# Windowed attention and a feed-forward block on one core: local units taken one by one, or in pairs

## The chip, the core and the metric

The program runs on one core of a Trainium2 chip. A core has a matrix engine (TensorE, in the profile PE, its weight loads PEld), a vector engine (VectorE, DVE), an engine for activation functions (ScalarE, ACT), a general one (GpSimd, POOL), and a queue from which all transfers of this program are issued (SyncE, SP; the transfers themselves are DMAs). Each engine works through its own list of instructions in order and waits at semaphores for the others. The metric is the device time of one execution in microseconds (us); lower is better.

## The reference

```python
# q_l, k_l, v_l: (8, 8, 512, 64); q_g, k_g, v_g: (8, 8, 32, 64), float32
def sm(s):
    e = np.exp(s - np.max(s, axis=-1, keepdims=True))
    return e / (np.sum(e, axis=-1, keepdims=True) + 1e-09)
k_all, v_all = concat([k_g, k_l]), concat([v_g, v_l])
out_g = sm(scale * q_g @ k_all.T) @ v_all               # 32 global rows see all 544
s_ll = np.where(abs(i - j) <= 32, scale * q_l @ k_l.T, -1e9)
a_l = sm(concat([scale * q_l @ k_g.T, s_ll]))           # 512 local rows see a band and the globals
out_l = a_l @ v_all
x = concat([out_g, out_l], axis=2).transpose(0, 2, 1, 3).reshape(8, 544, 512)
xn = (x - mean(x)) / sqrt(var(x) + 1e-06) * g_ln
return x + np.maximum(xn @ w_ch1, 0) @ w_ch2            # 512 -> 2048 -> 512
```

## The kernel before, in words

The feed-forward block (`ffn`) runs over nine chunks. Chunks 0 to 7 hold 512 local rows each (one batch), the last one the 256 global rows. A chunk goes through 16 slices f of the hidden layer. `mm1(f)` is 12 matrix products of 128 rows by 512 columns into a PSUM tile `ph` (each operand is split in a high and a low part, `xh`, `xl`, `w`; three of the four products are made); ScalarE then writes `hh` (L540, the high part of the rectified result) and VectorE `hl` (L541, the low part). `mm2(f - 1, t)` for four row tiles t is 12 more products from the `hh` and `hl` of the slice before into four accumulators `acc`. So a slice is 24 products, a chunk 384, and the `hl` of slice f is first needed after `mm1(f + 1)`.

The attention of the next chunk is pushed between these products. A unit (`Local`) is one batch, two heads and half of the local rows; a chunk needs 8 units. A unit's steps are: `scores`, small products into two tiles `sc` (L262; the trace counts 32 of them a unit, 64 rows by 32 columns of weights each); on VectorE a masked scaling and minimum (L275) and on ScalarE the exponential with its sum (L285), four of each; `transposes`, for the first 16 units on TensorE (L299 into `tp`, copied by ScalarE, L301), and from then on 16 transposes of 32-row blocks on VectorE (L307); `values`, 32 small products (L317) of which VectorE then writes the quotient into `x` (L328, L329). With the fourth pair of heads a half of the chunk is complete: `finish` stores the raw `x` to a buffer in memory (`xs`, L343), takes mean and variance (L189, L191, L193, L194), and ScalarE normalises `x` in place (L202), for which it has to wait until the store has read `x`. At the end of a chunk `transpose_chunk` brings the next chunk's normalised `x` through TensorE into `xh` and `xl` (L493, L505, L506), and `load_residual` fetches `xs` back for the sum at the end (L560, L582).

From the second chunk on the scores of unit u and the values of unit u - 1 stand together on TensorE; the values go to the free half of the tile that holds the scores. The 56 units that chunks 0 to 6 push in are placed by a table, `PLACES`: two places a slice (after `mm1` of the slice, or ahead of it), a first place, a period of 3.5 or 3.75 places, and an offset for each step. A generator `side` holds the steps; the loop of products calls `next(side, None)` seven times a slice, three times in `mm1` and ahead of each of the four row tiles.

The order on TensorE is the order in which the program is written, from chunk 0 on (`tc.manual_schedule`), and so it is for the transfers, apart from chunk 0. On VectorE, ScalarE and GpSimd a planner sets the order; it works from its own costs and lets what is under `hurry` go first, here chunk 0's `hh` and `hl`. Chunk 0's attention runs ahead of everything else, in the first 60 us (units with `alone` set). The weights are packed; VectorE and ScalarE unpack them (`split_weights`: L138, L139, L150 on ScalarE, L141, L142, L146, L152 on VectorE), three slices ahead of chunk 0's products. During chunk 7 the 8 global units (`Global`, L372 to L437) are pushed in, and the last chunk has nothing to push in.

A unit's keys, queries and values come in one transfer of 848 KB (L245), two units ahead.

Of the kernel before, what the change touches and what calls it, by code (L numbers as in the profile page):

```python
# [19 lines left out]
P = 128  # L20
# [12 lines left out]
ON_PE = 16  # L33

PLACES = {0: (0, 3.5, (0, 2, 3)), 7: (1, 3.5, (0, 1, 2)), 9: (1, 3.75, (0, 1, 4))}
# [11 lines left out]
def attention_ffn_kernel(  # L47
# [133 lines left out]
    def norm(x, js, xn=None):  # L181
# [13 lines left out]
        if xn is None:  # L195
            nc.vector.scalar_tensor_tensor(  # L196
                rs[:, 1, at], mv[:, at, 0], -1.0, rs[:, 0, at], ALU.mult, ALU.mult
            )
        def apply():
            for j in js:  # L200
# [19 lines left out]
    class Local:  # L220


        def __init__(self, b, hp, half, alone, on_pe):
            self.at = b, hp, half
            self.alone = alone
            self.on_pe = on_pe
            self.next = self.beside = None

        def bank(self, k, name):

            if not self.alone or k == 2:
                return ps_a.tile([P, 512], F32, name=name, tag="att")
            if k < 2:
                return ps_h.tile([P, 512], F32, name=name, tag="ph")
            return ps_o.tile([P, 512], F32, name=name, tag=f"acc{next(accs)}")

        def load(self, n=1):

            if self.alone:
                u = wpool.tile([P, 2 * (KT * P + DM)], F32, name="u", tag=UNITS[units.index(self)])  # L240
            else:
                u = self.ap.tile([P, eu.shape[4]], F32, name="u", bufs=2)
# [51 lines left out]
        def transposes(self):  # L294
            self.pt = self.ap.tile([P, 4, P], F32, name="pt", bufs=2)
            if self.on_pe:
                tp = self.bank(2, "tp")
                for c in range(4):
                    nc.tensor.transpose(tp[:, c * P:(c + 1) * P], self.p[:, c], ident)  # L299
                yield  # L300
                nc.scalar.copy(self.pt, tp.rearrange("p (c q) -> p c q", c=4))  # L301
                return
            for g in range(4):
                gp = slice(g * WIN, (g + 1) * WIN)
                for r in range(4):
                    rp = slice(r * WIN, (r + 1) * WIN)
                    nc.vector.transpose(out=self.pt[rp, :, gp], in_=self.p[gp, :, rp])  # L307

        def values(self):
            b, hp, half = self.at  # L310

            pv = self.beside.sc[0][:, 256:] if self.beside else self.bank(3, "pv")
# [22 lines left out]
            if not self.alone and self.next and self.next.next:  # L335
                self.next.next.load()

        def finish(self):
            b, hp, half = self.at
            if hp == HP - 1:  # L340
                for j in range(2):
                    r0 = b * SA + SG + half * 256 + j * P
                    nc.sync.dma_start(xs[r0:r0 + P, :], self.x[:, j, :])  # L343
                self.xn = new_x() if self.alone and half else None
                return norm(self.x, range(2), self.xn)
            return ()

# [92 lines left out]


# [70 lines left out]

    def ffn(c, xt, rows, stage, next_chunk):
# [11 lines left out]
        def mm1(f):  # L525
# [3 lines left out]
            for w, xx in ((w1l, xh), (w1h, xl), (w1h, xh)):  # L529
                next(side, None)  # L530
# [8 lines left out]
            with hurry(c == 0):  # L539
# [23 lines left out]
        side = iter(())  # L563
        for f in range(NF):
            side = chain(side, stage(f, 0))
            mm1(f)
            side = chain(side, stage(f, 1))
            if f == NF - 2:
                load_residual()
            if f == NF - 1:  # L570
                side = chain(side, next_chunk())
            for t in range(nt):
                next(side, None)
                if f > 0:
                    mm2(f - 1, t)
        for t in range(nt):
            next(side, None)
            mm2(NF - 1, t)
            if t == nt - 1:
                for _ in side:  # L580
                    pass
# [24 lines left out]
    for c, chunk in enumerate(chunks):  # L606
        if chunk is None:
            phases[1] += [Global(bg, hp) for bg in range(NBG) for hp in range(HP)]
        else:
            phases[0] += [  # L610
                Local(b, hp, half, c == 0, len(phases[0]) + hp < ON_PE)
                for b, half in chunk for hp in range(HP)
            ]
# [10 lines left out]
    traced = {"units": 0}  # L624
# [3 lines left out]
    def begin(phase):  # L628
# [9 lines left out]
        for a, b in zip(us, us[1:] + [None]):  # L638
            a.ap, a.next = ap, b
        if phase == 1:  # L640
# [6 lines left out]
    def values(u):  # L647
# [3 lines left out]
        if n == 0 or n % HP == 0 and u.chunk != last_chunk:  # L651
            got.append(new_x())
        u.x = got[-1]
        u.values()
        for p, us in enumerate(phases):
            if u is us[-1]:
                begin(p + 1)
        return u.finish()

    def stages(units):  # L660


        for n, u in enumerate(units):
            before = units[n - 1] if n else None
            if before and u.chunk == last_chunk and before.chunk < last_chunk:
                before = None
            alone = n + 1 == len(units) or u.chunk == last_chunk or units[n + 1].chunk == last_chunk

            def first(u=u, before=before):
                scores = u.scores()  # L670
                if before and u.chunk < last_chunk:
                    next(scores)
                    before.beside = u
                    for _ in values(before):
                        pass
                yield from scores

            def second(u=u):
                for _ in u.transposes():
                    pass  # L680
                return
                yield

            def third(u=u):
                for _ in values(u):
                    pass
                yield

# [173 lines left out]
```

## Time and profile before

| | |
|---|---|
| median of 3 runs | 982.0 us (978.03 to 983.02) |
| profiled execution, from the first to the last instruction | 981.9 us |
| TensorE busy / VectorE / ScalarE / GpSimd | 938.4 / 573.0 / 316.5 / 45.0 us |
| mean granted clock of TensorE | 0.975 |
| instructions | 21071 |

The page gives no other time for the profiled execution than its span, and no time around it. The span lies 0.1 us from the median of the runs. In the profile "L317" is line 317 of the kernel, "pv<-u,pt" says that `pv` is written from `u` and `pt`, an x with a number counts instructions, and what stands in square brackets is idle time ahead of an instruction with what ended it. One program product in full float32 counts as two in the trace.

### The profile page before, as it was taken

The page shows a single profiled execution, that of the slowest core. Times are in us where ns is not written, and L with a number is a line of the kernel's source. Part 1 is how long each engine was busy: PE and PEld are TensorE (multiplying, and loading weights), DVE is VectorE, ACT ScalarE, POOL GpSimd, SP SyncE. Part 2 cuts the span into 40 slices and gives each one's busy share as a digit, 9 for nine tenths or more (in the row PEclk, how much of TensorE's full clock was granted, in tenths as well). Part 3 has the DMA queues.
Part 4 walks back from the last instruction along what each step waited for, and adds up shares of the span by engine and source line. Part 5 has one row for each costly group of instructions (what it writes and reads, how often), then busy time and mean ns, then how long its engine had stood idle before and what let it go on. Part 6 is the DMA issues. An engine that isn't in the chain of part 4 may idle for free.

```text
span 981.9 us, 21071 instructions
## 1 busy us (share of the span) xinstructions
PE 938.4 (96%) x8616; PEld 723.1 (74%) x8616; DVE 573.0 (58%) x1873; ACT 316.5 (32%) x842; POOL 45.0 (5%) x150
## 2 busy tenths in 40 slices
PE   6669999999999999999999999999999989899997
PEld 4357777777777777777777777777777867576896
DVE  4589965666676766676676667666766442222311
ACT  5677843222322223232322232223222222222210
POOL 3000100000000000000000000000000000000000
PEclk9579999999999999999999999999999999989999
DMA  9575641332432232131422242223322434444210
GB/s 361 198 248 211 226 157 58 115 93 73 136 115 92 73 130 89 69 119 61 164 72 93 72 143 98 83 93 100 115 93 72 159 123 156 154 141 141 88 31 22
DMA packets 31872, 118.80 MB, mean 121 GB/s; under 512 B 4256, under 2 KB 6304, under 8 KB 27680
## 3 DMA queue, kind: packets, MB, share of 16 engines
q1 hardware_dynamic: 31776, 117.46, 34.7%
q8 instruction: 68, 1.11, 0.5%
q14 instruction: 28, 0.23, 0.1%
HBM read 99.62 MB, written 17.83 MB: 120 GB/s over the span
## 4 chain that ended last, share of the span: by engine, by line
PE 79%; DVE 9%; ACT 3%; DMA 2%; issue 1%; POOL 0%; SPq 0%; ACTq 0%; DVEq 0%
PE acc L551 35%; PE ph L532 34%; DVE pt L307 3%; PE sc L317 3%; PE sc L262 2%; PE t L493 1%; PE pv L420 1%; ACT p L285 1%; DMA raw<-in_wd 1%; DVE hl L541 1%; PE sc L372 1%; DVE tmp L142 1%; PE t L408 1%; DVE tmp L146 1%; DVE w L152 1%
## 5 line engine op out<-in xcount | busy, mean ns | idle before, releaser
L551 PE MATMUL acc<-w,hh 128*128 128x512 f32 x1088 | 343.2, 397 | 0.0
L532 PE MATMUL ph<-xh,w 128*128 128x512 f32 (+1 forms) x1216 | 312.9, 383 | 0.0
L307 DVE STREAM_TRANSPOSE pt<-p 32x128 f32<-32x128 f32 x768 | 232.1, 302 | 38.3 <-ACT p L285 27.0
L532 PEld LDWEIGHTS ph<-xh,w 128*128 128x128 f32 x1216 | 214.7, 189 | 48.9 <-issue 1.8
L551 PEld LDWEIGHTS acc<-w,hh 128*128 128x128 f32 x1088 | 206.0, 189 | 45.7
L541 DVE SCALAR_TENSOR_TENSOR hl<-ph,hh 128x512 fp32r<-128x512 f32 (+1 forms) x144 | 93.8, 651 | 232.0 <-ACT hh L540 231.9
L551 PE MATMUL acc<-w,hl 128*128 128x512 f32 x544 | 222.6, 409 | 0.5 <-DVE hl L541 0.5
L540 ACT ACTIVATE hh<-ph 128x512 fp32r<-128x512 f32 (+1 forms) x144 | 82.5, 573 | 403.0 <-PE ph L532 403.0
L532 PE MATMUL ph<-xl,w 128*128 128x512 f32 x512 | 142.0, 399 | 0.0
L285 ACT ACTIVATE p<-p,mn 128x128 f32<-128x128 f32 x256 | 100.2, 393 | 118.0 <-DVE mn L275 117.9
L551 PEld LDWEIGHTS acc<-w,hl 128*128 128x128 f32 x544 | 102.6, 189 | 26.5 <-issue 3.1
L532 PEld LDWEIGHTS ph<-xl,w 128*128 128x128 f32 x512 | 97.0, 190 | 25.5 <-issue 1.8
L275 DVE CUSTOM_DVE_ANT_0 p<-sc,mask 128x128 f32<-128x128 f32 x256 | 63.0, 285 | 46.2 <-PE sc L262 40.6
L262 PE MATMUL sc<-u 64*32 64x128 f32 x2048 | 49.6, 291 | 10.3 <-DMA u<-in_eu 4.4
L262 PEld LDWEIGHTS sc<-u 64*32 64x32 f32 x2048 | 29.4, 111 | 33.5 <-issue 25.1
L285 ACT ACTIVATION_READ_ACCUMULATOR p<-p,mn 128x1 f32 x256 | 48.0, 187 | 0.0
L327 POOL TENSOR_SCALAR ri<-sm 128x4 f32<-128x4 f32 x64 | 16.5, 258 | 669.9 <-ACT p L285 666.2
L202 ACT ACTIVATE x<-x,rs 128x512 f32<-128x512 f32 x32 | 24.5, 809 | 56.4 <-DVE rs L196 42.3
L317 PE MATMUL sc<-u,pt 128*32 128x64 f32 x1760 | 37.7, 222 | 3.8 <-DVE pt L307 3.8
L317 PEld LDWEIGHTS sc<-u,pt 128*32 128x32 f32 x1760 | 27.9, 109 | 15.7 <-issue 10.9
L493 PE MATMUL t<-ident,x 128*128 128x128 f32 x136 | 24.1, 295 | 10.1 <-DVE x L207 3.9
L493 PEld LDWEIGHTS t<-ident,x 128*128 128x128 f32 x136 | 17.0, 148 | 18.1 <-issue 6.8
(61 smaller groups left out, 477.3 us busy)
## 6 DMA issues: line engine op xcount, KB each, us to landing
u<-in_eu SPq DMA_DIRECT2D x63, 848.0 KB, 4.8
raw<-in_wd SPq DMA_DIRECT2D x16, 1024.0 KB, 5.3
gk<-in_gk SPq DMA_DIRECT2D x8, 1088.0 KB, 5.0
xs<-x SPq DMA_DIRECT2D x32, 256.0 KB, 5.4
ob<-xs SPq DMA_DIRECT2D x32, 256.0 KB, 5.3
out<-ob SPq DMA_DIRECT2D x32, 256.0 KB, 2.1
gv<-in_gv SPq DMA_DIRECT2D x8, 1024.0 KB, 5.1
u<-in_eu SPq DMA_DIRECT2D x1, 512.0 KB, 3.7
```

What stands on the lines that cost most here:

```text
L202: nc.scalar.activation(x[:, j, :], x[:, j, :], AF.Identity, bias=rs[:, 1, j:j + 1], scale=rs[:, 0, j:j + 1],)
L262: nc.tensor.matmul(sc[h][gp, qb * P:(qb + 1) * P], self.e[hd, w * WIN:(w + 1) * WIN], self.e[hd, k0 * WIN:(k0 + 4) * WIN], start=True, sto ...
L275: nc.vector.tensor_tensor_reduce(out=self.p[:, c], in0=sc[h][:, qb * P:(qb + 1) * P], in1=masks[half, qb], scale=-QSCALE, scalar=BIG, op0= ...
L285: nc.scalar.activation(self.p[:, c], self.p[:, c], AF.Exp, bias=mn[:, c:c + 1], scale=-1.0, accum_out=self.sm[:, c:c + 1],)
L307: nc.vector.transpose(out=self.pt[rp, :, gp], in_=self.p[gp, :, rp])
L317: nc.tensor.matmul(pv[gp, qb * P + h * D:qb * P + h * D + D], self.pt[:, 2 * h + qb, gp], self.v[:, 4 * qb + g, h * D:(h + 1) * D], start= ...
L327: nc.gpsimd.tensor_scalar(ri, self.sm, SUM_EPS, None, ALU.add)
L493: nc.tensor.transpose(t[:, j * P:(j + 1) * P], xn[j][:, kt * P:(kt + 1) * P], ident)
L532: nc.tensor.matmul(ph[:, :n], w[:, kt, :], xx[kt][:, :n], start=(i == 0), stop=(i == 3 * KT - 1),)
L540: nc.scalar.activation(hh[:, :n], ph[:, :n], AF.Relu)
L541: nc.vector.scalar_tensor_tensor(hl[:, :n], ph[:, :n], 0.0, f32(hh[:, :n]), ALU.max, ALU.subtract)
L551: nc.tensor.matmul(acc[t], a[:, ts], w, start=(f == 0 and i == 0), stop=(f == NF - 1 and i == 2),)
```

## The change

Chunk 0's attention ahead of the loop stays on single units, with its PSUM tiles moved: the scores take the two banks `att`, and the transposed scores an accumulator's bank. From the second chunk on there is a new class `Pair`: two neighbouring units (four heads) at once.

- Its scores fill both `sc` tiles whole, and its values fill a bank of their own, from the tag `ph` that `mm1` uses too. Keys with queries and values come in two transfers (`e` of 688 KB and `v` of 1024 KB, one buffer each), issued as soon as the pair before has been read.
- `attend(u, before, spread)` puts the scores of pair u and the values of the pair before next to each other, always between `mm1(f)` and `mm2(f - 1, 0)`, at f = 1, 5, 9 and 13 (`PAIR_STEPS`). In chunk 0 the five places are 6.5 places apart, and the transposes of a pair follow two places later on TensorE.
- In chunks 1 to 6 (`rest`) VectorE, ScalarE and GpSimd keep the order in which the program is written. The pair's 32 transposes on VectorE are written two at a time, one turn at each of the loop's seven steps a slice, so that `hl` of the following slices stands among them. The in-place normalisation is written at the steps 5 and 7 after the values of a completed half.
- `side` becomes a queue that is carried over the end of a chunk, and `transpose_chunk` goes ahead of what is left in it. `hh` and `hl` are under `hurry` in all chunks.
- The constructor of the program gets a smaller scratch space for GpSimd's transfers, of which there are none.

```diff
-PLACES = {0: (0, 3.5, (0, 2, 3)), 7: (1, 3.5, (0, 1, 2)), 9: (1, 3.75, (0, 1, 4))}
+PAIR_STEPS = (1, 5, 9, 13)
...
+    class Pair:
...
+        def scores(self):
...
+            sc = [self.bank("sc") for _ in range(2)]
+            for j in range(2):
+                for qb in range(2):
+                    for g in range(4):
...
+                            nc.tensor.matmul(
+                                sc[h][gp, at:at + P],
+                                self.e[hd, j, w * WIN:(w + 1) * WIN],
+                                self.e[hd, j, k0 * WIN:(k0 + 4) * WIN],
...
+            if self.next_pair:
+                self.next_pair.load_scores()
+            yield
+            for j in range(2):
+                if j:
+                    yield
...
+                        nc.vector.tensor_tensor_reduce(
...
+                        nc.scalar.activation(
...
+        def transposes(self):
...
+                        nc.vector.transpose(out=self.pt[rp, j, :, gp], in_=self.p[gp, j, :, rp])
+                        if r % 2:
+                            yield
+
+        def values(self):
+            b, hp, half = self.at
+            pv = ps_h.tile([P, 512], F32, name="pv", tag="ph")
...
+            nc.gpsimd.tensor_scalar(ri, self.sm, SUM_EPS, None, ALU.add)
+            if self.next_pair:
+                self.next_pair.load_values()
+            else:
+                begin(1)
+            yield
+            nc.vector.reciprocal(ri, ri)
...
+            yield
+            if hp == HP - 2:
+                store_x(b, half, self.x)
+                yield from norm(self.x, range(2))
...
+    def attend(u, before, spread):
+
+        sums = values(before) if before else iter(())
+        scores = u.scores() if u else iter(())
+        next(scores, None)
+        next(sums, None)
+        next(scores, None)
+        next(sums, None)
+        yield
+        for _ in scores:
+            yield
+        turns = u.transposes() if u and spread else iter(())
+        ends = before.at[1] == HP - 2 if before else False
+        n = 0
+        while True:
+            if ends and n in (0, 5, 7):
+                next(sums, None)
+            elif next(turns, turns) is turns:
+                break
+            n += 1
+            yield
+        for _ in sums:
+            pass
...
             if f == NF - 1:
-                side = chain(side, next_chunk())
+                if c in (0, last_chunk - 1):
+                    drain()
+                side.appendleft(next_chunk())
...
         if c == 1:
             ctx.enter_context(tc.manual_schedule(engines={ET.SP}))
+            rest = ExitStack()
+            rest.enter_context(tc.manual_schedule(engines={ET.DVE, ET.Activation, ET.Pool}))
+        if c == last_chunk - 1:
+            rest.close()
...
+        if c == 0:
+            for n in range(len(PAIR_STEPS) + 1):
+                u, before = new.pop(0)
+                put(1 + 6.5 * n, lambda u=u, before=before: attend(u, before, False))
+                put(3 + 6.5 * n, u.transposes)
+        elif c < last_chunk - 1:
+            for f in PAIR_STEPS:
+                u, before = new.pop(0)
+                put(2 * f + 1, lambda u=u, before=before: attend(u, before, True))
```

What this moves is seen in the lists of instructions of the two programs. On TensorE in the fourth chunk before, a single unit's scores (`sc<-u`) and the values of the one before (`sc<-u,pt`) stand between two slices' products:

```order
L551 MATMUL acc_4104<-w,hl 128x512
L551 MATMUL acc_4104<-w,hh 128x512 x2
L262 MATMUL sc<-u 32x128 x16
L317 MATMUL sc<-u,pt 32x64 x16
L532 MATMUL ph<-xh_4042,w 128x512 x2
L532 MATMUL ph<-xh_4064,w 128x512 x2
```

In the changed program at such a place, one chunk later:

```order
L673 MATMUL ph<-xh_5033,w 128x512 x2
L673 MATMUL ph<-xh_5055,w 128x512 x2
L378 MATMUL sc<-e 32x128 x32
L443 MATMUL pv<-v,pt_5499 32x64 x32
L692 MATMUL acc_5100<-w,hl 128x512
L692 MATMUL acc_5100<-w,hh 128x512 x2
```

Twice the small products stand at one place, the values in a tile of their own, and there are half as many such places.

On ScalarE before, in the same chunk, with the normalisation L202 between two `hh` late after the exponentials L285:

```order
L285 ACTIVATE p,sm<-p,mn 128x128 x4
L540 ACTIVATE hh<-ph 128x512 x2
L285 ACTIVATE p,sm<-p,mn 128x128 x4
L540 ACTIVATE hh<-ph 128x512
L202 ACTIVATE x<-x,rs 128x512 x2
L540 ACTIVATE hh<-ph 128x512
```

In the changed program (exponentials L407, normalisation L203, `hh` L681):

```order
L681 ACTIVATE hh<-ph 128x512 x4
L407 ACTIVATE p_4334,sm_4333<-p_4334,mn_4332 128x128 x8
L203 ACTIVATE x<-x,rs 128x512
L681 ACTIVATE hh<-ph 128x512
L203 ACTIVATE x<-x,rs 128x512
L681 ACTIVATE hh<-ph 128x512 x3
```

The first half of the normalisation has moved ahead of the next slice's `hh`, directly behind the pair's eight exponentials.

On ScalarE at the beginning of chunk 0 before, where the weights are unpacked (L138, L139, L150), L285 belongs to the first unit that is pushed in and L540 is the first `hh`:

```order
L505 ACTIVATE xh_605<-t,g_sb 128x256 x2
L138 ACTIVATE tmp<-raw 128x1024
L139 ACTIVATE raw<-raw 128x1024
L150 CAST w<-tmp 128x1024
L285 ACTIVATE p,sm<-p,mn 128x128 x3
L138 ACTIVATE tmp<-raw 128x1024
L285 ACTIVATE p,sm<-p,mn 128x128
L139 ACTIVATE raw<-raw 128x1024
L150 CAST w<-tmp 128x1024
L540 ACTIVATE hh<-ph 128x512
```

In the changed program (unpacking L137, L138, L149):

```order
L681 ACTIVATE hh<-ph 128x512
L137 ACTIVATE tmp<-raw 128x1024
L138 ACTIVATE raw<-raw 128x1024
L149 CAST w<-tmp 128x1024
L137 ACTIVATE tmp<-raw 128x1024
L407 ACTIVATE p_767,sm_766<-p_767,mn_765 128x128
L138 ACTIVATE raw<-raw 128x1024
L407 ACTIVATE p_767,sm_766<-p_767,mn_765 128x128 x7
L149 CAST w<-tmp 128x1024
L681 ACTIVATE hh<-ph 128x512
```

The eight exponentials of the first pair stand behind the first `hh` and, all but one, behind five instructions of unpacking.

More of the change, by code (lines that the diff above doesn't have):

```diff
@@ L1 @@
 from contextlib import ExitStack, nullcontext
+from collections import deque
 from itertools import chain, cycle
@@ L295, in transposes @@
             self.pt = self.ap.tile([P, 4, P], F32, name="pt", bufs=2)
[L296 to L307, printed above, removed]
+            tp = self.bank(2, "tp")
+            for c in range(4):
+                nc.tensor.transpose(tp[:, c * P:(c + 1) * P], self.p[:, c], ident)
+            yield
+            nc.scalar.copy(self.pt, tp.rearrange("p (c q) -> p c q", c=4))
         def values(self):
             b, hp, half = self.at
-            pv = self.beside.sc[0][:, 256:] if self.beside else self.bank(3, "pv")
+            pv = self.bank(3, "pv")
             for h in range(2):
@@ L340, in finish, with store_x @@
             if hp == HP - 1:
[L341 to L344, printed above, removed]
+                store_x(b, half, self.x)
+                self.xn = new_x() if half else None
                 return norm(self.x, range(2), self.xn)
             return ()
+    def store_x(b, half, x):
+        for j in range(2):
+            r0 = b * SA + SG + half * 256 + j * P
+            nc.sync.dma_start(xs[r0:r0 + P, :], x[:, j, :])
@@ L439, in attention_ffn_kernel @@
     class Global:
+        alone = True
         def __init__(self, bg, hp):
@@ L511, in attention_ffn_kernel, with step, drain @@
     out_flat = out.rearrange("b s d -> (b s) d")
+    side = deque()
+    def step():
+        while side:
+            if next(side[0], side) is not side:
+                return
+            side.popleft()
+    def drain():
+        while side:
+            for _ in side.popleft():
+                pass
     def ffn(c, xt, rows, stage, next_chunk):
@@ L576, in ffn @@
         for t in range(nt):
-            next(side, None)
+            step()
             mm2(NF - 1, t)
-            if t == nt - 1:
-                for _ in side:
-                    pass
+            if t == nt - 1 and c == last_chunk - 1:
+                drain()
             nc.vector.tensor_tensor(obs[t], acc[t], obs[t], op=ALU.add)
@@ L609, in attention_ffn_kernel @@
         else:
[L610 to L613, printed above, removed]
+            if c == 0:
+                phases[0] += [Local(b, hp, half) for b, half in chunk for hp in range(HP)]
+            else:
+                phases[0] += [
+                    Pair(b, hp, half, c == 1) for b, half in chunk for hp in range(0, HP, 2)
+                ]
         for u in sum(phases, []):
@@ L650, in values @@
         got = ready.setdefault(u.chunk, [])
-        if n == 0 or n % HP == 0 and u.chunk != last_chunk:
+        if n == 0 or u.at[1] == 0 and u.chunk != last_chunk:
             got.append(new_x())
         u.x = got[-1]
+        if not u.alone:
+            return u.values()
         u.values()
-        for p, us in enumerate(phases):
-            if u is us[-1]:
-                begin(p + 1)
+        if u is units[-1]:
+            begin(2)
         return u.finish()
[L660 to L687, printed above, removed]
-            yield (first, second, third) if alone else (first, second)
@@ L696, in attention_ffn_kernel, with global_stages, run, go @@
+    def global_stages(u):
+        def run(part):
+            def go():
+                yield from part()
+            return go
+        def sums():
+            for _ in values(u):
+                pass
+            yield
+        return u.scores, run(u.transposes), sums
     ET = mybir.EngineType
@@ L738, in attention_ffn_kernel @@
     ready.pop(0)
-    traced["units"] = need[0]
+    new = [(u, v) for u, v in zip(phases[0][need[0]:] + [None], [None] + phases[0][need[0]:])]
     for c, chunk in enumerate(chunks):
@@ L748, in attention_ffn_kernel, with put @@
             rows = [rows_local(b, 2 * half + j) for b, half in chunk for j in range(2)]
[L749 to L752 removed]
         at = {}
[L754 to L758 removed]
+        def put(place, run):
+            at.setdefault(min(int(place), 2 * NF - 1), []).append(run)
+        if c == 0:
+            for n in range(len(PAIR_STEPS) + 1):
[6 more added lines that the diff above has]
+                put(2 * f + 1, lambda u=u, before=before: attend(u, before, True))
+        elif c < last_chunk:
+            for n, u in enumerate(phases[1]):
+                for o, run in enumerate(global_stages(u)):
+                    put(1 + 3.5 * n + o, run)
         def stage(f, k, at=at, c=c):
```

155 lines of the change are left out of this document (116 added, 39 removed).

## The prediction

> **What bounds the kernel now.** I read the page's shares first, then a table by chunk, then the timeline of one insertion. From the page: the busy shares.
>
> ```profile
> PE 938.4 (96%) x8616; PEld 723.1 (74%) x8616; DVE 573.0 (58%) x1873; ACT 316.5 (32%) x842; POOL 45.0 (5%) x150
> ```
>
> TensorE is busy 96% of the span, so time is won only where its list gets shorter or a wait in it goes. Next the stretches chunk by chunk: chunk 0, 5, 6 and 7, with the span, each engine's busy time, and behind them the granted clock and the transfers' share and rate.
>
> ```profile
> core 0: us, PE busy (x) PEld busy (x) DVE busy (x) ACT busy (x) POOL busy (x), PEclk, DMA share, GB/s
> 59.31:172.42 113.11, 109.95 (x951) 84.62 (x945) 88.97 (x192) 71.21 (x140) 7.35 (x13) 0.98 0.51 175
> ...
> 586.00:689.36 103.36, 102.74 (x913) 80.32 (x912) 68.65 (x243) 28.62 (x88) 3.69 (x12) 1.00 0.29 99
> 689.36:792.14 102.78, 102.16 (x881) 79.92 (x880) 63.16 (x218) 26.98 (x80) 3.46 (x11) 1.00 0.32 105
> 792.14:895.40 103.26, 97.18 (x1031) 68.42 (x1030) 28.01 (x100) 25.60 (x55) 2.35 (x9) 0.95 0.46 156
> ```
>
> Chunks 5 and 6 are full on TensorE to within 0.7 us (and 1 to 4, of the same list, with them); VectorE has a third of each to spare. Now one ordinary insertion, and the one in each chunk that stalls (TensorE's timeline; the first column is the start, the second the length).
>
> ```profile
> 207.66 0.40 PE L551 MATMUL acc<-w,hl 128*128 128x512 f32 x1
> 207.90 0.63 PE L551 MATMUL acc<-w,hh 128*128 128x512 f32 x2
> 208.46 0.67 PE L262 MATMUL sc<-u 64*32 64x128 f32 x32
> 209.06 0.65 PE L317 MATMUL sc<-u,pt 128*32 128x64 f32 x32
> 209.64 1.20 PE L532 MATMUL ph<-xh,w 128*128 128x512 f32 x4
> 210.68 1.09 PE L532 MATMUL ph<-xl,w 128*128 128x512 f32 x4
> 211.61 0.40 PE L532 MATMUL ph<-xh,w 128*128 128x512 f32 x1
> ...
> 286.35 0.31 PE L317 MATMUL sc<-u,pt 128*32 128x64 f32 x6
> 287.28 0.63 PE L317 MATMUL sc<-u,pt 128*32 128x64 f32 x26 [0.62 <-DVE pt L307]
> ```
>
> Four dense products take 211.61 - 210.68 = 0.93, so one 0.233 and a chunk's 384 some 89.6 us. From 207.66 to 210.68 are 3.02 us with 7 dense products (1.63): an insertion costs 1.39; I use 1.37, since the 211.61 row shows the pitch only to a hundredth. In the second group the values stand 0.62 us for the transposes and start up a second time: 287.28 less (286.35 + 0.31) is 0.62, and the start-up adds some 0.3, so 2.29. A chunk then is 89.6 + 7 x 1.37 + 2.29 = 101.5, and 1.9 more for the transposition at its end, the 103.4 of the table.
>
> **A pair's insertion.** Instead of two insertions one has 64 scores and 64 values. The price of the second half comes from inside the groups; these rows of the page (behind the count stand the busy time and the mean ns of one) give the length of one.
>
> ```profile
> L307 DVE STREAM_TRANSPOSE pt<-p 32x128 f32<-32x128 f32 x768 | 232.1, 302 | 38.3 <-ACT p L285 27.0
> ...
> L541 DVE SCALAR_TENSOR_TENSOR hl<-ph,hh 128x512 fp32r<-128x512 f32 (+1 forms) x144 | 93.8, 651 | 232.0 <-ACT hh L540 231.9
> ...
> L285 ACT ACTIVATE p<-p,mn 128x128 f32<-128x128 f32 x256 | 100.2, 393 | 118.0 <-DVE mn L275 117.9
> ...
> L262 PE MATMUL sc<-u 64*32 64x128 f32 x2048 | 49.6, 291 | 10.3 <-DMA u<-in_eu 4.4
> ...
> L317 PE MATMUL sc<-u,pt 128*32 128x64 f32 x1760 | 37.7, 222 | 3.8 <-DVE pt L307 3.8
> ```
>
> First start to last start is 0.67 - 0.29 = 0.38 for the scores and 0.65 - 0.22 = 0.43 for the values. So 64 more products cost at least 0.8, and at most what they cost from start to start, 0.60 + 0.58 = 1.18, if every fill and drain is paid again. I take 0.88, near the lower end, since nothing inside a group changes when it goes on. A pair's insertion is 1.37 + 0.88 = 2.25 against 2.74 for two, 0.49 less (0.2 to 0.55).
>
> The Trainium skill, "TensorEngine Tiling (Array Packing)", Performance Considerations, speaks against this: every matmul on TRN2 carries about 60 cycles of overhead, which at 2.4 GHz would make an estimate of 64 x 25 ns = 1.6 us for the second half, 16 us more over 23 pairs, and a sum near 981. The trace disagrees with it for these packed tiles: 64 of them start and end within 208.46 to 209.71, 19.5 ns each.
>
> **Chunks 1 to 6.** The stalled insertion disappears: a pair's values come four slices after its scores, 25 us, and its 8 exponentials (8 x 0.39) and 32 transposes (32 x 0.30 = 9.7) are written over fewer than three slices. Chunks 1 to 5 each had 11.9 and get 4 x 2.25 = 9.0: 5 x -2.9 = -14.5. Chunk 6 had 6 x 1.37 + 2.29 + 0.78 (values alone) = 11.3 and gets 3 x 2.25 + 1.22 = 8.0: -3.3. Together -17.8.
>
> The edits that I cost at nothing, with what covers them. The order by hand on ScalarE and VectorE: after a pair's insertion the four `mm2` groups (2.8) and the next `mm1` (2.8) follow, and `hl` of the next slice is due only after a further `mm1` and `mm2`, so about 13.5 us after the end of this slice's `mm1`. Ahead of it VectorE has 8 masked scalings, the quotient and its share of transposes, about 12 of 0.3, and is done by 9; `hh` waits behind 8 exponentials to about 4.8. Both have 4 us to spare, where no normalisation stands ahead. Where one does, it waits for a store: the rival below. The transfers: the new `v` and `e` are asked for 22 us ahead of their use, and the DMA share of 0.3 leaves room. SyncE now issues two transfers a pair (0.33 us apiece) instead of two of `u`, with the stores behind them. GpSimd has its `ri` at most one place later, on 5% load. The smaller scratch space moves no instruction.
>
> Chunk 6 to 7: the loads for the global part (2.2 MB) now stand ahead of the last `xs` store, 0 to 1 us at the seam; I take 0.5. From chunk 7 on the instructions stand in the same order on every engine, so the 103.3 us of chunk 7 with this stall (first ScalarE's row, then TensorE's) stay, and what follows it:
>
> ```profile
> 856.71 0.81 ACT L202 ACTIVATE x<-x,rs 128x512 f32<-128x512 f32 x1 [8.94 <-DMA xs<-x]
> 859.14 1.52 PE L372 MATMUL sc<-gk,gq 64*32 64x272 f32 x16 [3.03 <-DVE gp L382]
> ```
>
> **Chunk 0 and its start.** First rows of TensorE's timeline, then ScalarE's unpacking by groups.
>
> ```profile
> 57.89 1.49 PE L262 MATMUL sc<-u 64*32 64x128 f32 x32 [3.77 <-DVE xl L506]
> 59.31 2.07 PE L532 MATMUL ph<-xh,w 128*128 128x512 f32 x4
> ...
> 100.82 0.93 PE L299 MATMUL tp<-ident,p 128*128 128x128 f32 x4 [1.40 <-ACT p L285]
> ```
>
> ```profile
> L138 ACT ACTIVATE tmp<-raw 128x1024 f32<-128x1024 f32 x16 | 18.4, 1159 | 6.3 <-DVE w L152 4.5 <-DMA raw<-in_wd 1.8
> L139 ACT ACTIVATE raw<-raw 128x1024 int32<-128x1024 uint16 x16 | 18.4, 1151 | 8.5 <-DMA raw<-in_wd 8.5
> L150 ACT CAST w<-tmp 128x1024 fp32r<-128x1024 f32 x16 | 16.8, 1051 | 5.6 <-DVE tmp L146 5.3
> ```
>
> The first scores no longer stand ahead of `mm1(0)`, nor take a bank that waits 3.77 us for `xl`; `mm1(0)` needs `xl` too, but only for its products with `xl`, so I let it start 3.4 earlier (0 to 4). Eight insertions (11.6) become four pairs and one scores-only (10.2): -1.4. The waits of chunk 0 that go with single units add up to 2.3 (the 1.40 above, and 0.9 in smaller ones of 0.3 to 0.4). Against this the first pair's transposes on TensorE, one `mm1` and one `mm2` after its scores, find its exponentials behind an `hh` (0.6) and five unpackings (3.36 + 1.16 + 1.15 = 5.7): with the 8 x 0.39 = 3.1 they are done 9.4 after the scores, where TensorE has 4.0 of other work. That is 5.4 if the whole set is awaited and 3.9 for its first half; I take 4.2. A wait of this size also costs clock. The later three pairs wait 0 to 3 each; I take 0.5 apiece, 1.5.
>
> ```profile
> 796.90:800.30 3.40, 1.81 (x21) 0.84 (x22) 1.57 (x8) 1.74 (x5) 0.10 (x1) 1.00 0.34 87
> 800.30:803.70 3.40, 3.40 (x11) 2.82 (x12) 0.22 (x2) 1.00 (x2) 0.13 (x1) 0.50 0.57 241
> ```
>
> The clock stands in the third column from the right: after a window in which TensorE was busy for 1.81 us of 3.40, the next ran at 0.50. A wait of 4.2 leaves a window of 3.4 less busy than 1.8, so I add one window at half clock: 1.4 (11 dense products in 3.40 would be 2.57 at full clock, 0.8; by twice the pitch 1.7; I take nearer the second). The Trainium skill, "TensorE: Matmul & The Clock Gate", Part 1, asks for a whole idle window of about 3.4 us, free-running. By that rule a 4.2 us wait would mostly cost no clock, and the sum would be 1.4 lower; the first row disagrees with it.
>
> Chunk 0 and its start: -3.4 - 1.4 - 2.3 + 4.2 + 1.4 + 1.5 = 0.0 (-5 to +8).
>
> **The sum** against the profiled execution, whose span of 981.9 is the median of 982.0 but for 0.1: 981.9 - 17.8 + 0.0 + 0.5 = 964.6.
>
> **The rivals.**
> - Chunk 0 pays at all four pairs (about 973). If each later pair's exponentials, too, stand behind one unpacking of 3.36, the three wait 2.2 each instead of 0.5, 5.1 more, and with two more windows at half clock, 2.8, it is 972.5. For it: the 1.40 at 100.82 with a single unit. Against: unpacking ends as chunk 0 goes on.
> - Slower: the in-place normalisation waits for the `xs` store, and now the next slice's `hh` stands behind it. This row of the table by stretches, with one `u` on its way, gives the rate.
>
> ```profile
> 211.00:216.00 5.00, 5.00 (x23) 4.05 (x22) 4.79 (x17) 0.93 (x3) 1.17 (x3) 1.00 0.81 267
> ```
>
> The store is issued 3.0 after the slice's `mm1`, behind `e` and `v` (1.7 MB) issued from 1.3 on: 1.97 MB at 267 GB/s from 2.6 lands at 10.0. With 0.8 for the normalisation, 0.6 and 0.65 for `hh` and `hl`, `hl` is there at 12.0, due at 13.5. From a landing at 11.5 on, each us costs a us at the twelve completed halves; slower by over 5 it is from 13.4 on (23 / 12 = 1.9 past the deadline), at 987. For it: the 8.94 above for the same instruction, which cost TensorE 3.03. Against: 3.4 us of error in a sum whose largest term is 7.4.
> - The second half of an insertion pays everything again, 1.37 as the first: then only the six stalls (6 x 0.92 = 5.5) are saved of 17.8, and the time is 977, at the edge of no change. The rows inside the groups speak against it. The Trainium skill's rule on a matmul's overhead, cited above, would bring the time past this one.
> - A pair's 128 small products in a row outrun the fetching of instructions. One idle 0.41 of a unit's scores is put down to "issue":
>
> ```profile
> 23.17 1.12 PE L262 MATMUL sc<-u 64*32 64x128 f32 x32 [0.41 <-issue]
> ```
>
> 28 pairs x 0.41 give 976. It stands once, in the start.
> - More gain, 958: the start's 4 us in full, no wait in chunk 0 but the first half's 3.9, no lost clock, and 0.55 a pair.
>
> **How the numbers follow.** What a measurement of this kernel can tell from no change is about 0.5%, 4.9 us, the spread of its three runs: faster is below 977.1, slower above 986.9. Forecast (959 to 970): 0.68. All four pairs wait: 0.13. More gain: 0.06. Store late: 0.05, of which 0.04 slower. Second half at full price: 0.04, no change. Fetching: 0.04, at the edge. That is faster 0.89 with nearly all of the first three and half of the last, no change 0.07, slower 0.04. The range goes from the more-gain case, less 1, to the fetching case, 957 to 977; it leaves out the late store, half of the full price and the tails.
>
> **What the changed profile would show.** Right: 2.2 to 2.3 per pair between dense products; chunks of 100.5 with no wait for `pt`; the first product of `mm1` before 57; one wait of about 4 for exponentials by the first transposes in chunk 0. Wrong: a wait of the products with `hl` in the slices behind a completed half, and in the same place ScalarE's normalisation waiting for `xs`; a group of 64 scores longer than 1.3; more than one window of chunk 0 at half clock.

## The result and the profile after

| | before | changed |
|---|---|---|
| median (lowest to highest) of 14 runs | 978.9 us (976.2 to 983.0) | 987.4 us (979.6 to 993.6) |
| ratio, 95% interval | | 1.0071 (1.0046 to 1.0096) |
| profiled execution, span | 981.9 us | 987.1 us |

The changed kernel is 0.7% slower; 964.6 was forecast. From its page, the busy shares, the granted clock (one digit for each fortieth of the span, in tenths of full speed) and the chain that ended last (the work followed back from the last instruction):

```profile
PE 933.2 (95%) x8616; PEld 732.2 (74%) x8616; DVE 571.0 (58%) x1845; ACT 312.9 (32%) x842; POOL 38.4 (4%) x122
PEclk9769998999999998999999999999999999999999
PE 76%; DVE 9%; DMA 9%; ACT 4%; issue 2%; SPq 0%; POOL 0%; ACTq 0%; DVEq 0%
```

TensorE is busy 5 us less, and the span is 5 us longer. Of the chain, transfers have 9% (2% before), and the store `xs` alone 5%. The next table of stretches has chunks 0, 1, 2, 6, and the chunk of the global units as far as the prediction's row went (columns as in the table of before):

```profile
50.95:179.01 128.06, 117.48 (x1012) 91.75 (x1013) 99.59 (x217) 77.31 (x155) 6.12 (x9) 0.90 0.48 173
179.01:281.26 102.25, 100.87 (x914) 80.64 (x912) 64.54 (x229) 28.23 (x88) 2.83 (x8) 1.00 0.29 99
281.26:388.19 106.93, 103.78 (x913) 82.84 (x912) 69.12 (x240) 28.16 (x88) 2.83 (x8) 0.97 0.28 97
...
702.19:802.37 100.18, 99.91 (x849) 79.73 (x848) 60.17 (x200) 24.96 (x72) 2.58 (x7) 1.00 0.29 100
802.37:905.63 103.26, 99.28 (x1124) 70.61 (x1123) 28.28 (x101) 25.61 (x55) 2.33 (x9) 0.98 0.47 159
```

Chunk 2 has 3 us of TensorE idle and a clock of 0.97; before, no chunk from 1 to 6 had lost more than 0.7 us or any clock. By the starts of the first product of each chunk, the two profiled executions differ so:

| | before | changed | difference |
|---|---|---|---|
| up to chunk 0's first product | 59.3 | 51.0 | -8.4 |
| chunk 0 | 113.1 | 128.1 | +14.9 |
| chunks 1 to 6 | 619.7 | 623.4 | +3.6 |
| chunk 7 | 138.1 | 133.2 | -5.0 |
| global rows | 51.6 | 51.6 | 0.0 |
| sum | 981.9 | 987.1 | +5.2 |

Against the forecast's terms that is 20.9 us more in chunks 1 to 6 (+3.6 for -17.3), 6.6 more in chunk 0 with its start, and 5.0 less in chunk 7: together the 22.5 between 964.6 and 987.1.

The insertion itself is what was forecast. One in chunk 2 on TensorE's timeline:

```profile
358.23 1.10 PE L673 MATMUL ph<-xh,w 128*128 128x512 f32 x4
...
361.13 1.16 PE L378 MATMUL sc<-e 64*32 64x128 f32 x64
362.21 1.10 PE L443 MATMUL pv<-v,pt 128*32 128x64 f32 x64
363.25 0.50 PE L692 MATMUL acc<-w,hl 128*128 128x512 f32 x1
...
366.16 1.09 PE L673 MATMUL ph<-xh,w 128*128 128x512 f32 x4
...
371.74 1.10 PE L673 MATMUL ph<-xh,w 128*128 128x512 f32 x4
```

The slice with the pair lasts 366.16 - 358.23 = 7.93, the one behind it 5.58, so the pair costs 2.35 (2.33 over all slices; 2.25 forecast). What is lost stands in each chunk's last slice, from the first product of `mm1(15)` to that of the next chunk:

| last slice of chunk | 0 | 1 | 2 | 3 | 4 | 5 | 6 |
|---|---|---|---|---|---|---|---|
| before | 11.3 | 10.2 | 10.2 | 10.2 | 10.2 | 10.2 | 10.3 |
| changed | 16.8 | 11.8 | 16.5 | 15.8 | 11.8 | 14.8 | 10.3 |

In chunks 1 to 5 that is 1.5 + 6.2 + 5.6 + 1.5 + 4.6 = 19.4 us. Chunk 2's end, engine by engine: SyncE, ScalarE, VectorE, TensorE.

```profile
362.36 0.37 SPq L353 DMA_DIRECT2D e<-in_eu  x1
363.38 0.37 SPq L357 DMA_DIRECT2D v<-in_eu  x1
364.39 1.19 SPq L335 DMA_DIRECT2D xs<-x  x2
```

```profile
373.09 0.82 ACT L203 ACTIVATE x<-x,rs 128x512 f32<-128x512 f32 x1 [6.83 <-DMA xs<-x]
373.81 0.57 ACT L681 ACTIVATE hh<-ph 128x512 fp32r<-128x512 f32 x1
```

```profile
369.05 0.16 DVE L198 SCALAR_TENSOR_TENSOR rs<-mv,rs 128x2 f32<-128x2 f32 x1
374.42 0.69 DVE L682 SCALAR_TENSOR_TENSOR hl<-ph,hh 128x512 fp32r<-128x512 f32 x1 [5.21 <-ACT hh L681]
375.14 3.79 DVE L430 STREAM_TRANSPOSE pt<-p 32x128 f32<-32x128 f32 x12
378.96 0.69 DVE L682 SCALAR_TENSOR_TENSOR hl<-ph,hh 128x512 fp32r<-128x512 f32 x1
379.57 1.40 DVE L634 SCALAR_TENSOR_TENSOR xl<-t,g_sb,xh 128x512 fp32r<-128x512 f32 x2
```

```profile
380.37 1.12 PE L621 MATMUL t<-ident,x 128*128 128x128 f32 x4 [3.06 <-DVE xl L634]
```

Read from above: the store is issued behind 1.7 MB of loads (672 KB of `e` and 1024 KB of `v` by the page); ScalarE is idle for 6.83 us ahead of the in-place normalisation of `x`, and from 369.2 on, when its statistics (`rs`) are there, it waits for the store alone, 3.9 us; `hh(14)` stands behind the normalisation on ScalarE and `hl(14)` waits for `hh(14)`. VectorE, idle for 5.21 us, then does `hl(14)` just in time for TensorE. But twelve transposes, written between `hl(14)` and `hl(15)`, begin only now, and `hl(15)` and the `xl` of the chunk's transposition stand behind them. The third group of transpositions on TensorE needs the PSUM bank that the first `xl` has to read. The Trainium skill, "PSUM — Partial Sum Buffer", Engine vs sequencer instructions, says that VectorE's and ScalarE's queues are strictly first in, first out; these rows agree: 3.8 us of ready work stood in front of the instructions that TensorE waited for.

Before, at the end of the same chunk, VectorE had its transposes behind it when `hl(14)` came, and nothing stood between `hl(14)` and `hl(15)`:

```profile
365.93 2.52 DVE L307 STREAM_TRANSPOSE pt<-p 32x128 f32<-32x128 f32 x8
...
368.62 0.69 DVE L541 SCALAR_TENSOR_TENSOR hl<-ph,hh 128x512 fp32r<-128x512 f32 x1
372.72 0.69 DVE L541 SCALAR_TENSOR_TENSOR hl<-ph,hh 128x512 fp32r<-128x512 f32 x1 [3.42 <-ACT hh L540]
373.33 0.74 DVE L506 SCALAR_TENSOR_TENSOR xl<-t,g_sb,xh 128x512 fp32r<-128x512 f32 x1
```

The wait costs twice. The granted clock around it (third column from the right):

```profile
377.00:380.40 3.40, 0.34 (x3) 0.04 (x1) 3.29 (x10) 0.34 (x1) 0.00 (x0) 0.85 0.00 0
380.40:383.80 3.40, 3.40 (x12) 2.95 (x13) 1.32 (x2) 0.83 (x2) 0.00 (x0) 0.50 0.02 5
```

Over the run, the waits of TensorE for `xl`, and of ScalarE for the store:

```profile
PE t L621 <- DVE xl L634: 11.7, 5, 3.1
...
ACT x L203 <- DMA xs<-x: 76.2, 13, 7.3
```

Five waits of 11.7 us stand against 19.4 us lost at the five chunk ends; most of the rest is half clock behind three of them (0.97 or 0.98 in the means of chunks 2, 3 and 5, which is 6.8 us in all; 1.00 in chunks 1 and 4).

### The profile page after: what moved, and what is told of

It reads as the page before. It is cut to its first block, busy times and chain, and to the rows that moved or that the text cites. A ratio compares the mean times of both kernels' runs of the same rounds, so it can differ in the third digit from the quotient of the medians.

```text
span 987.1 us, 20917 instructions
## 1 busy us (share of the span) xinstructions
PE 933.2 (95%) x8616; PEld 732.2 (74%) x8616; DVE 571.0 (58%) x1845; ACT 312.9 (32%) x842; POOL 38.4 (4%) x122
## 4 chain that ended last, share of the span: by engine, by line
PE 76%; DVE 9%; DMA 9%; ACT 4%; issue 2%; SPq 0%; POOL 0%; ACTq 0%; DVEq 0%
PE acc L692 33%; PE ph L673 33%; DMA xs<-x 5%; DVE pt L430 3%; DMA raw<-in_wd 3%; PE pv L443 2%; PE sc L378 2%; PE pv L547 1%; DVE hl L682 1%; PE t L621 1%; ACT hh L681 1%; PE sc L499 1%; DVE p L397 1%; DMA u<-in_eu 1%; PE t L535 1%
## 5 line engine op out<-in xcount | busy, mean ns | idle before, releaser
L692 PE MATMUL acc<-w,hh 128*128 128x512 f32 x1088 | 347.2, 401 | 0.0
L430 DVE STREAM_TRANSPOSE pt<-p 32x128 f32<-32x128 f32 x768 | 232.1, 302 | 11.3
L692 PE MATMUL acc<-w,hl 128*128 128x512 f32 x544 | 226.6, 417 | 0.3 <-DVE hl L682 0.3
L681 ACT ACTIVATE hh<-ph 128x512 fp32r<-128x512 f32 (+1 forms) x144 | 82.2, 570 | 447.0 <-PE ph L673 447.0
L407 ACT ACTIVATE p<-p,mn 128x128 f32<-128x128 f32 x224 | 87.2, 391 | 27.5 <-DVE mn L397 27.5
L203 ACT ACTIVATE x<-x,rs 128x512 f32<-128x512 f32 x32 | 25.5, 810 | 90.1 <-DMA xs<-x 76.2
L397 DVE CUSTOM_DVE_ANT_0 p<-sc,mask 128x128 f32<-128x128 f32 x224 | 50.8, 284 | 0.0
L621 PE MATMUL t<-ident,x 128*128 128x128 f32 x136 | 26.6, 318 | 22.6 <-DVE xl L634 11.7
L407 ACT ACTIVATION_READ_ACCUMULATOR p<-p,mn 128x1 f32 x224 | 42.0, 187 | 0.0
L633 ACT ACTIVATE xh<-t,g_sb 128x512 fp32r<-128x512 f32 (+1 forms) x40 | 24.6, 621 | 31.0 <-PE t L621 30.8
L634 DVE SCALAR_TENSOR_TENSOR xl<-t,g_sb,xh 128x512 fp32r<-128x512 f32 (+1 forms) x36 | 24.1, 687 | 16.0 <-ACT xh L633 15.9
L378 PEld LDWEIGHTS sc<-e 64*32 64x32 f32 x1792 | 25.5, 107 | 10.5 <-issue 10.5
L378 PE MATMUL sc<-e 64*32 64x128 f32 x1792 | 33.2, 279 | 0.0
L443 PE MATMUL pv<-v,pt 128*32 128x64 f32 x1792 | 30.8, 220 | 0.0
```

Source lines behind the costliest of these rows:

```text
L203: nc.scalar.activation(x[:, j, :], x[:, j, :], AF.Identity, bias=rs[:, 1, j:j + 1], scale=rs[:, 0, j:j + 1],)
L378: nc.tensor.matmul(sc[h][gp, at:at + P], self.e[hd, j, w * WIN:(w + 1) * WIN], self.e[hd, j, k0 * WIN:(k0 + 4) * WIN], start=True, stop=Tr ...
L397: nc.vector.tensor_tensor_reduce(out=self.p[:, j, c], in0=sc[h][:, at:at + P], in1=masks[half, qb], scale=-QSCALE, scalar=BIG, op0=ALU.add ...
L407: nc.scalar.activation(self.p[:, j, c], self.p[:, j, c], AF.Exp, bias=mn[:, j, c:c + 1], scale=-1.0, accum_out=self.sm[:, j, c:c + 1],)
L430: nc.vector.transpose(out=self.pt[rp, j, :, gp], in_=self.p[gp, j, :, rp])
L443: nc.tensor.matmul(pv[gp, at:at + D], self.pt[:, j, 2 * h + qb, gp], self.v[:, j, 4 * qb + g, h * D:(h + 1) * D], start=True, stop=True, t ...
```

## The experiments

Four variants of the changed kernel ran first. In all, a slice's length is taken from the starts of the dense products, as above. The ratios are to runs of the kernel before that were made beside each set: 978.9 us beside the result, 980.9 beside these four, 981.0 beside the last four.

**The transposes away from the chunk's end.** The turns of the last pair of a chunk are written two or three at a time ahead of `hl(14)`, where VectorE idles, and none between `hl(14)` and `hl(15)`. The edit also writes the first half of the normalisation two steps earlier:

```diff
+        last = ends and before.at[2] == 1 and spread
+        sched = {1: 2, 2: 2, 4: 3, 5: 3, 6: 0, 8: 0, 9: 0, 10: 0, 11: 0, 12: 0} if last else {}
         while True:
-            if ends and n in (0, 5, 7):
+            if ends and n in ((0, 3, 7) if last else (0, 5, 7)):
                 next(sums, None)
-            elif next(turns, turns) is turns:
-                break
+            else:
+                got = [next(turns, turns) for _ in range(sched.get(n, 1))]
+                if turns in got:
+                    break
```

> Changed: only the place of 12 of the 32 VectorE transposes at the end of chunks 1 to 5. They stand ahead of the last slice but one's hl instead of between it and the last slice's hl. Theory 1 (the chain store -> normalise -> hh(14) -> hl(14) -> 12 transposes of 3.8 us -> hl(15) -> xl makes TensorE wait at the chunk's end): the waits of TensorE for xl (11.7 us in the changed kernel) go to under 2, the last slices come back from 11.8-16.5 to about 10.3 us, and the time falls by about 19 us to 968. Theory 2 (the late store alone makes the wait; the order on VectorE does not matter): the waits stay, 984 to 990.

Measured: 969.2 us, ratio to before 0.9893 (0.9872 to 0.9915), where the changed kernel had 1.0071. Chunks 1 and 5:

```profile
178.18:279.00 100.82, 100.82 (x914) 80.71 (x912) 64.65 (x229) 28.24 (x88) 2.84 (x8) 1.00 0.30 100
...
582.29:683.03 100.74, 100.74 (x914) 80.66 (x913) 68.46 (x239) 28.32 (x88) 2.83 (x8) 1.00 0.29 102
```

TensorE has no idle time left in these two; the last slices of chunks 1 to 5 are 10.3 to 10.7, and no wait for `xl` is left. Twelve transposes a chunk, moved by one slice, were worth 18 us. Theory 2 falls: the stores took 6.9 us to land, as late as in the changed kernel, and in three of the five chunks the normalisation started 11.7 to 12.1 us after the end of `mm1(13)`, as late as in the changed kernel's chunk 2 (11.9). So it was the transposes' place that told, and not the normalisation's.

**The stores ahead of the loads.** The other end of the same chain (`late` marks a pair whose scores stand next to the values that complete a half; `loads()` fetches the next pair's `v`):

```diff
-            if self.next_pair:
+            if self.next_pair and not self.late:
                 self.next_pair.load_scores()
...
+            if ends:
+                store_x(b, half, self.x)
+                u = self.next
+                if u and u.late and u.next_pair:
+                    u.next_pair.load_scores()
+                loads()
             yield
-            if hp == HP - 2:
-                store_x(b, half, self.x)
+            if ends:
                 yield from norm(self.x, range(2))
```

> Changed: at a completed half the two stores of x are issued ahead of the next pair's two loads instead of behind them. Theory 1 (a chain of which the late store is the first link): the store lands some 3 us sooner, the 12 transposes are through before the last slice's hl can start, and most of the 19 us go as well, 968 to 974. Rival (VectorE's order alone is the cause, the store has slack): the time stays within 4 us of the changed kernel's 987. A third possibility is that the loads come too late for the next pair: a wait of TensorE for e or v, over 990.

Measured: 965.6 us (965.1 to 967.2), ratio 0.9851 (0.9832 to 0.9869). The stores' median time from issue to landing, in the changed kernel and here, and then ScalarE and VectorE at chunk 2's end here:

```profile
xs<-x SPq DMA_DIRECT2D x32, 256.0 KB, 7.0
```

```profile
xs<-x SPq DMA_DIRECT2D x32, 256.0 KB, 2.6
```

```profile
365.79 0.82 ACT L203 ACTIVATE x<-x,rs 128x512 f32<-128x512 f32 x1 [2.98 <-DVE rs L198]
```

```profile
367.12 0.69 DVE L694 SCALAR_TENSOR_TENSOR hl<-ph,hh 128x512 fp32r<-128x512 f32 x1 [1.37 <-ACT hh L693]
367.84 3.78 DVE L431 STREAM_TRANSPOSE pt<-p 32x128 f32<-32x128 f32 x12
371.99 0.69 DVE L694 SCALAR_TENSOR_TENSOR hl<-ph,hh 128x512 fp32r<-128x512 f32 x1 [0.36 <-ACT hh L693]
```

The normalisation now waits for its statistics and no longer for the store. The twelve transposes stand where the changed kernel has them, but they begin early enough: `hl(15)` waits 0.36 us for its `hh`, and no longer behind them. Every chunk from 1 to 5 lasts 100.7 us, as the prediction had it (100.5). So the loss is one chain with two links, each necessary: with either gone the wait goes. The loads, at chunk 2's end issued 2.4 and 3.0 us later after `mm1(13)`, made TensorE wait nowhere. The Trainium skill, "DMA: Bandwidth & Descriptors", Queues, rings and completion order, says that each transfer engine takes its descriptors in ring order; 7.0 against 2.6 us for the same 256 KB agrees with that.

**The planner's order in chunks 1 to 6.**

```diff
-            rest.enter_context(tc.manual_schedule(engines={ET.DVE, ET.Activation, ET.Pool}))
```

> Changed: VectorE, ScalarE and GpSimd are ordered by the planner in chunks 1 to 6 as before; pairs, tiles and places as in the changed kernel. Theory 1: the planner lets hl and xl go ahead of transposes, so the chunk ends cost 10.3 us again and the time is about 968. Rival (the pairs themselves cost the time, whoever orders): 985 or more, with waits of the values for the transposes.

Measured: 1031.7 us, ratio 1.0521 (1.0499 to 1.0543). Theory 1 falls. The rival's bound of 985 holds, but not the waits that it named. TensorE's longest waits there:

```profile
PE acc L692 <- DVE hl L682: 24.5, 18, 2.0
PE t L621 <- ACT x L203: 22.8, 13, 3.5
```

The planner sets 19 of a pair's transposes ahead of the end of a half's statistics, so the normalisation comes late (ScalarE is idle for 95.0 us ahead of it, in 13 places, with the statistics as what came last), and TensorE waits for `x` at the chunk ends; and it waits for `hl` in three slices of every chunk. The order by hand as a whole is not what made the change slow: without it the pairs cost 44 us more. What it had wrong in chunks 1 to 5 is the chain at the chunk ends.

**Chunk 0: the transposes of a pair later.**

```diff
-                put(3 + 6.5 * n, u.transposes)
+                put((5 if n < 4 else 3) + 6.5 * n, u.transposes)
```

> Changed: in chunk 0 the first four pairs' transposes on TensorE come four places after their scores instead of two. Prediction's reading (they wait for exponentials that stand behind unpacking on ScalarE): the wait of 2.99 + 1.09 us in chunk 0's second slice and the half clock behind it go, 5 us less, about 982. Rival (ScalarE is behind by itself there, TensorE then waits for hl or xh instead): no more than 2 us less.

Measured: 988.4 us, ratio 1.0089 (1.0064 to 1.0114), no gain; the rival was right. In the changed kernel TensorE waits in chunk 0's second slice for the first pair's exponentials (first fence); here it waits as long, one slice on, for `hl(1)` (second fence):

```profile
67.91 0.33 PE L422 MATMUL tp<-ident,p 128*128 128x128 f32 x1 [2.99 <-ACT p L407]
69.33 1.25 PE L422 MATMUL tp<-ident,p 128*128 128x128 f32 x3 [1.09 <-ACT p L407]
```

```profile
69.20 1.19 PE L422 MATMUL tp<-ident,p 128*128 128x128 f32 x4
74.41 0.79 PE L692 MATMUL acc<-w,hl 128*128 128x512 f32 x1 [4.01 <-DVE hl L682]
```

The reason stands on VectorE and ScalarE of the changed kernel: the scores are done at 61.8, but the first masked scaling (VectorE) starts only at 66.23, behind the unpacking of weights, and `hh` of the second slice (ScalarE) only at 72.44, behind the eight exponentials and the unpacking that stands among and behind them:

```profile
65.09 1.23 DVE L151 TENSOR_TENSOR w<-tmp,w 128x1024 fp32r<-128x1024 f32 x1 [0.33 <-ACT w L149]
66.23 0.28 DVE L397 CUSTOM_DVE_ANT_0 p<-sc,mask 128x128 f32<-128x128 f32 x1
```

```profile
72.44 0.58 ACT L681 ACTIVATE hh<-ph 128x512 fp32r<-128x512 f32 x1
```

The chunk ends, which this edit leaves as they were, lost 2.2 to 5.3 us each here, 21.2 in all, so the 19.4 of the changed kernel's profile come again in a second run.

Four more kernels ran on another chip. The kernel before, once more:

> The kernel before once more, for a second profile. In chunk 7 its eighth slice took 14.0 us, in the changed kernel and in four variants 9.4 to 9.8. Theory 1 (the landing of the global part's stores varies from run to run): 9 to 10 us here, and a time of some 978. Rival (a property of the program before): 14 us again, and some 982.

Measured: 977.5 us, span 975.7, and 9.9 us for that slice; chunk 7 lasts 132.4 us instead of 138.1. ScalarE's wait there was 7.36 instead of 8.94:

```profile
853.14 0.81 ACT L202 ACTIVATE x<-x,rs 128x512 f32<-128x512 f32 x1 [7.36 <-DMA xs<-x]
```

So the 5.0 us that chunk 7 seemed to win are no gain of the change: two executions of the kernel before differ by as much. That the store's landing, 1.6 us later, cost TensorE 4 us in that slice fits these rows; it is one run against one, on two chips. The profiled execution of before was the longest of its 14 runs, which is most of why the medians differ by 8.5 us and the two profiles by 5.2.

**The order by hand from chunk 0's last three slices on** (stores first as well), its last pair spread like the others, and what is left of its turns carried over the end of the chunk:

```diff
+            if c == 0 and f == PAIR_STEPS[-1]:
+                ctx.enter_context(tc.manual_schedule(engines={ET.SP}))
+                rest.enter_context(tc.manual_schedule(engines={ET.DVE, ET.Activation, ET.Pool}))
...
-                put(1 + 6.5 * n, lambda u=u, before=before: attend(u, before, False))
-                put(3 + 6.5 * n, u.transposes)
+                put(1 + 6.5 * n, lambda u=u, before=before, n=n: attend(u, before, n == 4))
+                if n < 4:
+                    put(3 + 6.5 * n, u.transposes)
```

> Changed, with the stores first as well: the order by hand on VectorE, ScalarE and GpSimd begins with the last three slices of chunk 0, and the last pair of that chunk is spread over the steps as in the chunks behind it. Theory (the planner's order, 30 transposes ahead of the half's statistics, makes chunk 0's last slice 16.8 us): it falls to 10.3, and the time from 965.6 to 959. Rival (the last slice waits for the store or for unpacking): the time stays within 2 us of 965.6.

Measured: 961.8 us, ratio 0.9808 (0.9787 to 0.9828). The last slice of chunk 0 in the changed kernel and here:

```profile
162.25:179.01 16.76, 13.08 (x53) 10.23 (x52) 10.94 (x27) 4.75 (x7) 0.94 (x2) 0.80 0.02 8
```

```profile
161.14:171.39 10.25, 10.25 (x53) 8.26 (x52) 8.53 (x21) 3.24 (x5) 0.00 (x0) 1.00 0.27 103
```

The theory holds in the slice, 6.5 us; of the total 3.8 show, since in this profile chunk 0 begins 1.1 us later and chunk 7 takes 1.3 longer than with the stores first alone.

**Chunk 0's insertions later** (stores first as well):

```diff
-                put(1 + 6.5 * n, lambda u=u, before=before: attend(u, before, False))
-                put(3 + 6.5 * n, u.transposes)
+                put(5 + 5.5 * n, lambda u=u, before=before: attend(u, before, False))
+                put(7 + 5.5 * n, u.transposes)
```

> Changed, with the stores first as well: chunk 0's five insertions come at the places 5, 10.5, 16, 21.5 and 27 instead of 1, 7.5, 14, 20.5 and 27. Theory (the first pair's masked scalings stand on VectorE behind the unpacking, which bounds chunk 0's first 30 us whatever is pushed in): the wait for the exponentials in the second slice goes, but it comes back in later slices; no more than 3 us of the 965.6 are won. Rival (only the first pair's place is wrong): 5 to 6 us less, 960.

Measured: 964.3 us (960.6 to 964.9), ratio 0.9824 (0.9801 to 0.9847), 1.3 less than 965.6 by the medians. Chunk 0's first three slices take 21.8 us instead of 29.6, its slices 3 to 14 together 82.3 instead of 79.1, so two fifths come back in the slices into which the insertions moved; chunk 0 as a whole is 4.3 shorter in the profile. That is between the two expectations (3 and 5 to 6), and the spread of these runs does not let the medians decide.

**All three together.**

> All three together: stores first, the order by hand from the last three slices of chunk 0, and chunk 0's insertions later. By the theories 957 to 959; by the rival on the first pair's place 953 to 955.

Measured: 955.7 us (954.9 to 957.9), ratio 0.9747 (0.9727 to 0.9767). Chunk 0 and chunk 1 of it:

```profile
50.73:165.05 114.32, 111.40 (x1013) 87.00 (x1013) 94.84 (x207) 77.07 (x155) 4.85 (x9) 0.96 0.52 192
165.05:265.78 100.73, 100.73 (x913) 80.69 (x912) 68.45 (x239) 28.25 (x88) 2.83 (x8) 1.00 0.28 102
```

With the order by hand in both, the medians differ by 6.1 us (961.8 to 955.7), but in the profiles chunk 0 is shorter by 4.6 (118.9 to 114.3); the rest lies in its start and in chunk 7. With the 4.3 above, the later insertions are worth 4 to 5 us, between the two expectations, and the total lies between them too; how much of it is the first pair's place alone stays open. This version beats both kernels: 2.5% less than before.

## Why the prediction was wrong

- **The step that failed: the chunk's end was not in the sum.** Among the edits costed at nothing, the order by hand was given "4 us to spare", and the late-store rival was measured only by `hl` of the next slice: no loss up to a landing 11.5 us after `mm1`, slower from 13.4 on. By that measure the reckoning was near. The landing was put at 10.0; at the ends of chunks 1 to 5 the normalisation started 9.9 to 12.4 after the end of `mm1(13)`, and in chunk 2 `hl(14)` came at 13.9, just as TensorE took it. After the first half of a chunk, where other slices follow, the normalisation started as late (9.8 to 11.7), and that cost at most 0.5 us a time. But at the second half the next thing behind `hl` is not another slice with the same slack: twelve transposes, `hl(15)` and `xl` follow on VectorE, and TensorE's transposition needs `xl`. There the loss begins with a start of the normalisation at about 8.5: TensorE waited 1.4 for a start at 9.9 (chunk 1) and 2.8 for one at 11.4 (chunk 5), and with the stores first, at 8.1, `hl(15)` had 0.36 to spare. The rival was given a chance of 0.05, and the chain cost 19.4 us. Of the signs of being wrong, the normalisation's wait for `xs` showed; the products with `hl` waited 0.3 us in all, since the wait stood at `xl`.
- **The insertions: right.** 2.33 measured, 2.25 forecast; the stalls for `pt` are gone. With the store in front, chunks 1 to 6 took 603.3 us against 619.7 before, 16.4 less where 17.8 less 0.5 were forecast. That this version's 965.6 comes within 1 us of the 964.6 is in part luck: in its profile chunk 0 and its start cost 4.6 instead of 0.0, and chunk 7 took 5.0 less than in the profile from which the sum starts.
- **Chunk 0 and its start: mis-sized, +6.6 for 0.0.** It starts 8.4 earlier instead of 3.4. Of the 14.9 that the chunk then takes longer, the first two slices have 12.0 (25.1 instead of 13.1): the wait of 4.1 for exponentials was foreseen in size (4.2), but named after ScalarE's unpacking alone, while VectorE's holds the masked scalings up as well, and the first slice itself waited for the operands of its early start (1.8 us for `xh` alone). Between the first pair's scores and its transposes TensorE had one `mm1`, 3.1 us, and not the 4.0 with an `mm2` that were reckoned, so the size came out near in part by luck. The mean granted clock of these two slices was 0.64 (0.86 before). Another 5.5 are in the last slice, where the planner set 30 transposes around the last half's statistics, and which the order by hand brought back to 10.3; the prediction had no term for that. The slices between took 2.5 less.
- **The clock: right in kind, and worth more than it got.** One window at half clock was reckoned in all; chunk 0 had a mean clock of 0.90 (0.98 before), and three chunk ends lost some: behind waits of about 3 us, and not behind those of 1.4.
- **Chunk 7: unchanged in its instructions, but not fixed in time.** The same list took 138.1 and 132.4 us in two runs of the kernel before.
- **The second half of an insertion at full price, and instruction fetching: not seen.** No wait of a pair's products is put down to "issue", and no slice with a pair, undisturbed, took over 7.93.

## What to carry to other kernels

When instructions are put into a fixed order, follow for each engine not only the next instruction that somebody waits for but the one after it too: work that is ready but not urgent, written between two urgent instructions, is harmless while the first is on time and becomes the critical path when it is late. Issue a store that somebody waits for ahead of loads that nobody needs for 20 us; here that alone was worth 22 us. And where a wait only changes its name when its consumer is moved, as in chunk 0, look for the engine that is behind and move the work that it is given.

## What the runs showed of the hardware

A store of 256 KB took 7.0 us from issue to landing (the median of 32) with most of them behind 1.7 MB of loads from the same queue, and 2.6 us with those of chunks 1 to 6 ahead of the loads. TensorE's clock was 0.50 in the 3.4 us behind a wait of 3.06 us, and lost nothing behind waits of 1.4. And 64 more of the small products in a row cost less than the first 64: a pair's 128 take 2.33 us where a unit's 64 take 1.37, so 15 ns for each further one, and no wait of these products is put down to "issue".
